# Reordering the head loads of a dense-GELU forward and backward kernel: one load queue, the activation table first, a split first run

## The chip, the cores and the metric

The kernel runs on one core of one Trainium2 chip. The metric is device microseconds of the whole program, the median of several executions. The profile's span, from the first to the last recorded instruction, is a little shorter than that time.

## The reference

One dense layer with a GELU, a second dense layer, and the gradients of both:

```python
h   = einsum("bsd,df->bsf", x, w1) + b1
out = einsum("bsf,fd->bsd", gelu_tanh(h), w2) + b2
out, vjp = jax.vjp(f, x, w1, b1, w2, b2)
return out, *vjp(grad_out)
```

Here x and grad_out are 1 x 2048 x 448, w1 is 448 x 1792 and w2 is 1792 x 448, all in bf16. The six results are the output and the gradients of x, w1, b1, w2 and b2.

## The kernel before, in words

The 2048 rows of x form four blocks of 512, and the 1792 hidden columns form seven pairs of 2 x 128 columns, so there are 28 units of (block, pair). For each unit TensorE makes u = x w1 (steps named `u<unit>.<half>`) and q = grad_out w2^T (`q`), ScalarE and VectorE make gelu, its derivative and their products, and TensorE then adds up the output (`p`, `o`) and the gradient of x (`x`). After the four blocks the gradients of w1 and w2 follow (lines 839 and 893).

Nothing is scheduled at run time: the order of each engine's work is written out by hand in `PE_ORDER`, `ACT_ORDER`, `DVE_ORDER` and `SP_ORDER` (lines 91 to 133), and the semaphores come from what each instruction reads and writes. TensorE works on two halves of its rows at once: a `run` is a list of slots, and each slot is a pair of matmuls of 64 rows each.

The head is the stretch before the first u steps flow. Its names:

- `W6` (lines 386 to 390): six matmuls of 128 x 512 on a constant, without use for the result. `F6` (lines 392 to 395): six slots of 128 columns on a constant, likewise.
- `xr01`, `xr12`, `xr24` (`LXN`, line 597): loads of x's row tile 0, of tile 1, and of tiles 2 and 3 (each tile 128 rows of 896 bytes) into a buffer of the TR group. They are plain loads; x's first block is turned by TensorE.
- `ident` (`identity`, line 602): VectorE builds a 128 x 128 identity from counted numbers, with four constants that GpSimd writes (`identz`, line 724).
- `X0` to `X3` on TensorE (`XT`, line 617): the turn of one x tile against the identity, four slots of 64 columns. `X<t>.<i>` on ScalarE and VectorE (`XC`, line 630) copies a turned half tile out of PSUM into xT.
- `L0` to `L4` (`LW1`, line 644): column parts of w1's first 384 rows; parts 0 to 3 have 256 columns, and part 4 the rest. Part 1 is loaded in two pieces, `L1a` and `L1b`. `Z0` to `Z2` (`LW1Z`, line 649) load w1's last 128 rows, by columns, into a spare area of gh_nat. `K0` to `K3` load w2, `b1` loads the bias, and `X1` in `SP_ORDER` is the transposing load of x's second block.
- `S0` (line 268): unit 0 for x's tiles 0 and 1. It is three runs one behind the other: `second(0), second(1)` (two slots), `first(0..3)` (four slots), `second(2)` (one slot), each slot 256 columns wide. The last slot of `first` and the slot of `second(2)` read the Z0 area.
- `T1` (line 716): the first half of unit 0 for x's tiles 2 and 3, one tile of 128 columns after the other. `B`: a small matmul for the bias, between S0 and T1. `k0A k0B` and `c0..` add up unit 0's pieces and take them out of PSUM. Then come `u1.1 h1.2 u1.2 u2.1 u3.1 ...`.

Two queues load in the head. ScalarE issues `xr12`, `L0` and `Z0`, and loads its Gelu table behind them (`table`, line 765). SyncE issues `xr01`, `xr24`, `b1`, `L1a`, `L1b`, `Z1`, `L2`, `L3` and so on. A hand-written dependency (`HOLD`, line 554) makes the issue of `L1a` wait until the identity has been built; all of SyncE's later issues stand behind it.

Of the kernel before, what the change touches and what calls it, by code (L numbers as in the profile page):

```python
# [9 lines left out]
ALU = mybir.AluOpType  # L10
BF16 = mybir.dt.bfloat16
F32 = mybir.dt.float32
# [76 lines left out]


PE_ORDER = """
W6 X0 X1 F6 X2 X3 S0 B T1 u1.1 h1.2 u1.2 u2.1 u3.1 u2.2 u3.2 p0.0 p0.1 p0.2 p0.3 p1.0 p1.1 p1.2 u4.1 u5.1 u4.2
u5.2 p1.3 p2.0 p2.1 p2.2 p2.3 u6.1 p3.0 u6.2 p3.1 p3.2 p3.3 p4.0 p4.1 u7.1 p4.2 u7.2 p4.3 p5.0 p5.1 p5.2 p5.3 u8.1
p6.0 u8.2 q0.1 p6.1 q0.2 u9.1 p6.2 u9.2 q1.1 p6.3 q1.2 u10.1 o1.0.0.6.1 u10.2 q2.1 o1.1.0.6.1 u11.1 q2.2 u11.2
o1.0.0.6.2 o1.1.0.6.2 q3.1 u12.1 q3.2 u12.2 o1.0.6.10.1 q4.1 o1.1.6.10.1 u13.1 q4.2 u13.2 o1.0.6.10.2 q5.1 o1.1.6.10.2
# [11 lines left out]
x3.1.6.10.1 x3.0.6.10.2 x3.1.6.10.2 x3.0.10.14.1 x3.1.10.14.1 x3.0.10.14.2 x3.1.10.14.2  # L107
"""
ACT_ORDER = """
xr12 L0 Z0 table X0.1 X1.1 X2.0 X3.0 k0A k0B c0A1 s0 g0 s1 g1 c2B t0 s2 g2 g3 s3 c5B g4 t1 t2 c6B g5 g6 s4 s5 g7 c8A c8B g8 c9A c9B  # L110
g9 c10A c10B t3 t4 g10 s6 c11A c11B s7 g11 t5 c12A c12B g12 s8 t6 c13A c13B g13 s9 t7 s10 t8 c14A c14B t9 g14 s11 s12
c15A c15B t10 g15 c16A c16B s13 t11 g16 c17A c17B s14 t12 g17 c18A c18B s15 g18 vx0.2 c19A c19B t13 t14 g19 s16 c20A
c20B s17 g20 t15 s18 t16 s19 c21A c21B t17 g21 c22A c22B s20 t18 g22 c23A c23B g23 s21 t19 s22 t20 s23 c24A c24B t21
# [12 lines left out]
vx3.3  # L126
"""
SP_ORDER = """
xr01 xr24 b1 L1a L1b Z1 L2 L3 K0 K1 L4 Z2 K2 K3 X1 R F b2 Y0 J0 J1 J2 Y1 I0 E J3 I1 So0.1 So0.0 X2 H0 H1 H2 H3 H4 H5 H6 H7 H8 H9
T0 T1 H10 T2 H11 T3 H12 T4 H13 T5 So1.0 So1.1 T6 T7 H14 T8 Y2 H15 T9 X3 H16 T10 H17 Sx0.0 Sx0.1 T11 H18 H19 T12 H20  # L130
T13 T14 T15 So2.0 Y3 H21 So2.1 T16 H22 H23 T17 T18 T19 H24 Sx1.0 T20 Sx1.1 H25 T21 H26 Nx H27 T22 T23 Sx2.0 Sx2.1 T24
T25 T26 So3.0 So3.1 Ng T27 Sx3.0 Sx3.1
# [28 lines left out]
def make_plan(tc, ctx, x, w1, b1, w2, b2, grad_out, out_0, out_1, out_2, out_3, out_4, out_5):  # L161
    nc = tc.nc
    P = 128
    _, S, D = x.shape
    F = w1.shape[1]
    NS, NF, SB = S // P, F // P, 512
# [7 lines left out]
    g2 = grad_out.rearrange("b s d -> (b s) d")  # L174
# [11 lines left out]
    w1_sb = w1f[:, 0:4 * F].rearrange("p (k f) -> p k f", k=4)  # L186
# [6 lines left out]
    xT = [sb.tile([P, 4, EDGE + SB], BF16, name=f"xT{i}") for i in range(2)]  # L193
# [14 lines left out]
    stage = [sb.tile([P, 2, D], BF16, name=f"st{i}") for i in range(NST)]  # L208
# [12 lines left out]
    pl = Plan()  # L221


    DEP = mybir.DependencyInfo(mybir.DependencyClass.Sync, mybir.DependencyReason.DATA)
# [21 lines left out]
        for i in (0, 1):  # L246
            tail_of[slots[-1][i][0], i] = (n_run[0], m, idle)

    def uq_run(w, t, banks, pair, d, c0=0, c1=SB, at=0):

        ft = (2 * (pair % NPB), 2 * (pair % NPB) + 1)

        def plain(i, k, low, st, sp, banks=banks):
            rows = slice(0, 64) if low else slice(64, 128)
            cols = slice(ft[i] * P, (ft[i] + 1) * P)
            return (banks[i], (at, c1 - c0), w[rows, k, cols] if k < 3 else w1z[rows, cols], t[rows, k, EDGE + c0:EDGE + c1], st, sp)

        if w is w1_sb and pair < NPB and d < 3:
            if d == 1:
                run([(plain(1, k, True, k + at == 0, False), plain(0, k, False, k + at == 0, False)) for k in (0, 1, 2, 3)])
            else:
                run([(plain(0, k, True, False, k == 2), plain(1, (0, 1, 3)[k], False, False, k == 2)) for k in (0, 1, 2)])
            return

        if d == 3:
            one_, two = banks[:2], banks[2:]

            def first(k):
                return [plain(1, k, True, k == 0, k == 3, one_), plain(0, k, False, k == 0, k == 3, one_)]

            def second(k):
                return [plain(0, k, True, k == 0, k == 2, two), plain(1, (0, 1, 3)[k], False, k == 0, k == 2, two)]

            run([second(0), second(1)])
            run([first(k) for k in range(4)])
            run([second(2)])
            return  # L280

        def half(i, k, low, st, sp):
            rows = slice(0, 64) if low else slice(64, 128)
            early = not low and k == 3
            a, b = EDGE + c0 - early, (0 if w is w1_sb else EDGE - early) + ft[i] * P
            return (banks[i], c1 - c0, w[rows, k, b:b + P], t[rows, k, a:a + c1 - c0], st, sp)

        if d == 1:
            run([(half(1, k + 1, True, k == 0, False), half(0, k, False, k == 0, False)) for k in (0, 1, 2)])
        else:  # L290
            run([(half(0, k, True, False, k == 3), half(1, k, False, False, k == 3)) for k in (0, 1, 2, 3)])
# [20 lines left out]
    def pe(name, fn, reads, writes, cost, pat):  # L312
        o = pl.op("PE", name, fn, reads, writes, cost)
        o["pat"] = pat
        return o
# [13 lines left out]
    def part_w1(p):  # L329
        return ("w1", W1_PART[p % NPB])  # L330

    def U(p, d, hf=None, by_tile=False):
        b = p // NPB
        if hf is None:
            bk, hs, c, tag = u_banks(p), (0, 1), (0, SB), ""
            vs = [bank(("u", p, 0), bk[0]), bank(("u", p, 1), bk[1])]
        else:
            bk, hs, c, tag = ((4, 5), (0, 1))[hf], (hf,), (256 * hf, 256 * hf + 256), f"h{hf}"
            vs = [bank(("u", p, 0, hf), bk[0]), bank(("u", p, 1, hf), bk[1])]
            if d == 3:  # L340
                bk = bk + (6, 7)
                vs += [bank(("ux", p, 0), 6), bank(("ux", p, 1), 7)]
        rd = [part_w1(p)] + [("xT", b, h) for h in hs] + ([("w1z", REST[p])] if b == 0 else ["w1r"])
        if d == 2 and b > 0:
            rd += [("xe", b), "w1f"]
        def fn():
            for a in range(c[0], c[1], P) if by_tile else (c[0],):
                uq_run(w1_sb, xT[b % 2], bk, p, d, a, a + P if by_tile else c[1], a - c[0])

        pe(f"u{p}.{d}{tag}", fn, rd, vs,  # L350
           ("s512" if hf is None else "s256", 2 + d), (bk, d))

    def Q(p, d):
# [169 lines left out]
    for i, t in enumerate([t for t in SP_ORDER.split() if t[0] == "S"]):  # L523
        b, half = t[2:].split(".")
# [25 lines left out]
    def dq(eng):  # L550
        return {"SP": nc.sync, "ACT": nc.scalar, "POOL": nc.gpsimd}[eng]

    loads = {}
    HOLD = {"w11m0": "ident"}

    def dma(eng, name, out, in_, reads, writes, nbytes):
        def fn():
            d = loads[name] = dq(eng).dma_start(out=out, in_=in_)
            if name in HOLD:
                tc.add_manual_dep(d.ins, loads[HOLD[name]].ins.name, DEP, reason="behind the identity")  # L560
        pl.op(eng, name, fn, list(reads) + (["ident"] if name in HOLD else []), writes, ("dma", nbytes, "plain"))

    def dmaT(name, out, in_, reads, writes, nbytes, eng="SP"):
        pl.op(eng, name, lambda: dq(eng).dma_start_transpose(out=out, in_=in_), reads, writes, ("dma", nbytes, "turn"))
# [26 lines left out]

    x_rows = TR[NTR - 1][:, :, :, :].rearrange("p a h s -> p (a h) s")
    ident = stage[0][:, 0, 0:P]
    nums, turned, nums128 = stage[1][:, 0, 0:16], stage[1][:, 0, 32:64], stage[1][:, 0, 128:256]
    row, block = [stage[1][:, 1, 2 * i:2 * i + 2].bitcast(F32) for i in (0, 1)]

    def LXN(t0, t1, eng="SP"):

# [2 lines left out]

    def identity():

        nc.vector.memset(nums[:, 0:1], 0.0)
        for i in range(4):
            n = 1 << i
            nc.vector.tensor_scalar(out=nums[:, n:2 * n], in0=nums[:, 0:n], scalar1=float(n), scalar2=None, op0=ALU.add)
        low = nums[:, None, 0:16].to_broadcast([P, 8, 16])
        high = nums[:, 0:8, None].to_broadcast([P, 8, 16])
        nc.vector.scalar_tensor_tensor(out=nums128.rearrange("p (a b) -> p a b", a=8), in0=high, scalar=16.0, in1=low, op0=ALU.mult, op1=ALU.add)  # L610
        nc.vector.transpose(out=turned, in_=nums128[:, 0:32])
        nc.vector.tensor_scalar(out=row, in0=turned[:, 0:1], scalar1=block, scalar2=None, op0=ALU.add)
        loads["ident"] = nc.vector.tensor_scalar(out=ident, in0=nums128, scalar1=row, scalar2=None, op0=ALU.is_equal)

    X_BANKS = ((0, 1), (2, 3), (0, 1), (2, 3))

# [74 lines left out]
    def num(t):  # L691
        return [int(i) for i in t.split(".")]

    for t in PE_ORDER.split():
        k, a = t[0], t[1:]
        if k == "w":
            wake(int(a), P)
        elif k == "W":
            wake(int(a))
        elif k == "X":  # L700
            XT(int(a))
        elif k == "f":
            fill(int(a), (3, 2), 2 * P)
        elif k == "F":
            fill(int(a), (6, 7), 2 * P)
        elif k == "B":
            pe("b1u", lambda: nc.tensor.matmul(bk_(5)[:, 256:272], lhsT=b1n[0:64, :], rhs=ident[0:64, 0:16], start=True, stop=True,  # L707
                                               skip_group_check=True), ["b1n", "b1z", "ident"], [val(("b1u",), ("bank5b",))], ("s16", 1), (None, 0))
        elif k == "d":
            DM(*num(a))  # L710
        elif k == "h":
            hf, d = num(a)
            U(0, d, hf)
        elif k == "S":
            U(0, 3, int(a))
        elif k == "T":
            U(0, 1, int(a), True)
        elif k in "uqp":
            {"u": U, "q": Q, "p": OP}[k](*num(a))
        else:  # L720
            b, half, f0, f1, d = num(a)
            UN(k, b, half, list(range(f0, f1)), d)
# [214 lines left out]
```

## Time and profile before

| what | value |
|---|---|
| time, median of 3 runs | 264.4 us (264.23 to 264.69) |
| span of the profiled execution | 262.2 us |
| TensorE busy | 258.8 us (99%) |
| VectorE busy | 199.5 us (76%) |
| ScalarE busy | 127.6 us (49%) |
| bytes moved by DMA | 46.61 MB, mean 178 GB/s |

The profiled execution has no time listed beside its span; the median of the runs lies 2.2 us above the span. In the timeline a row says when a merged group of instructions begins and how long it lasts, then engine, line, operation, the tile written and the tiles read, and the count. An entry in square brackets is the idle time before it and what ended it. Rows that end in q (SPq, ACTq) are the issuing of DMAs, not their transfer.

### The profile page before, as it was taken

Reading aid. Unit: us, or ns where it says so; the run is one execution under the profiler, and the core shown is the slowest. Engines: PE = TensorE matmul, PEld = TensorE weight load, DVE = VectorE, ACT = ScalarE, POOL = GpSimd, SP = SyncE. Lnnn points to the kernel's source line nnn. Section 1 sums busy time; section 2 is a strip of 40 time slices with the busy share of each in tenths; the row PEclk is TensorE's granted clock in tenths of the full one; section 3 lists DMA queues with packets and bytes.
Section 4 is the critical chain, followed back from the end, with each engine's and each line's share of the span. In section 5 each row is a group of like instructions: output and inputs, shape, how many; then the busy total and the mean of one; then the engine's idle time right before and its main releaser. Section 6 shows DMA issues by size and latency. Waiting matters only on the chain.

```text
span 262.2 us, 5415 instructions
## 1 busy us (share of the span) xinstructions
PE 258.8 (99%) x2217; PEld 149.5 (57%) x2217; DVE 199.5 (76%) x287; ACT 127.6 (49%) x166; POOL 14.2 (5%) x11
## 2 busy tenths in 40 slices
PE   8999999999999999999999999999999999999995
PEld 5444455555555666666666677765555555555554
DVE  5999398999989989999997995249999999310000
ACT  5899569936898956875896310011121111000001
POOL 1000000000000000000000000000000392400000
PEclk9999999999999999999999999999999999999999
DMA  6999989999999892972487824974899999975221
GB/s 201 292 249 171 197 127 197 258 341 212 244 180 220 236 228 43 195 203 43 107 203 257 216 42 63 262 211 106 162 217 136 184 213 171 235 152 158 72 70 35
DMA packets 120633, 46.61 MB, mean 178 GB/s; under 512 B 96686, under 2 KB 120479, under 8 KB 120608
## 3 DMA queue, kind: packets, MB, share of 16 engines
q1 hardware_dynamic: 119920, 45.82, 78.0%
q10 hardware_dynamic: 688, 0.44, 0.6%
q8 instruction: 17, 0.28, 0.4%
q14 instruction: 8, 0.07, 0.1%
HBM read 8.20 MB, written 14.28 MB: 86 GB/s over the span
## 4 chain that ended last, share of the span: by engine, by line
PE 99%; ACT 0%; issue 0%
PE bank L242 48%; PE qb L242 18%; PE bank L839 16%; PE bank L893 16%; PE qb L389 1%; ACT w_sb L898 0%; PE bank L707 0%
## 5 line engine op out<-in xcount | busy, mean ns | idle before, releaser
L242 PEld LDWEIGHTS <-HG 64*128 64x128 bf16 x896 | 55.7, 94 | 32.2 <-POOLq L236 2.1
L242 PE MATMUL qb<-gT,w2Tf 64*128 64x512 bf16 x392 | 52.9, 376 | 0.0
L242 PE MATMUL bank<-w_sb,HG 64*128 64x448 bf16 x448 | 48.4, 349 | 0.0
L242 PE MATMUL bank<-xT,w1f 64*128 64x512 bf16 (+2 forms) x361 | 47.3, 368 | 0.0
L242 PE MATMUL bank<-w1T_sb,HG 64*128 64x448 bf16 x448 | 47.2, 349 | 0.0
L515 DVE SCALAR_TENSOR_TENSOR HG<-TR,qb 128x1024 bf16<-128x1024 bf16 x28 | 34.1, 1217 | 12.6 <-PE qb L242 12.6
L893 PE MATMUL bank<-w2Tf,HG 128*128 128x448 bf16 (+2 forms) x240 | 42.6, 340 | 0.0
L839 PE MATMUL bank<-w1f,gh_nat 128*128 128x448 bf16 x224 | 42.5, 352 | 0.0
L893 PEld LDWEIGHTS <-HG 128*128 128x128 bf16 x240 | 22.9, 98 | 19.8
L839 PEld LDWEIGHTS <-gh_nat 128*128 128x128 bf16 x224 | 21.8, 98 | 20.6 <-issue 0.4
L242 PEld LDWEIGHTS <-w2Tf 64*128 64x128 bf16 x392 | 24.1, 94 | 16.6 <-POOLq L236 0.3
L500 ACT ACTIVATE TR<-TR 128x1024 bf16<-128x1024 bf16 x28 | 29.2, 1052 | 6.6 <-DVE TR L490 6.6
L242 PEld LDWEIGHTS <-w1f 64*128 64x128 bf16 x388 | 22.0, 94 | 17.3 <-POOLq L236 0.7
L862 DVE TENSOR_TENSOR w1T_sb<-w1T_sb,gh_nat 128x1792 f32<-128x1792 f32 x14 | 28.4, 2025 | 0.5
L844 ACT ACTIVATE TR<-bank 128x448 bf16<-128x448 f32 x14 | 7.6, 543 | 34.9 <-PE bank L839 34.9
L899 DVE CAST w_sb<-bank 128x448 bf16<-128x448 f32 x6 | 3.7, 624 | 25.9 <-PE bank L893 25.9
L898 ACT CAST w_sb<-bank 128x448 bf16<-128x448 f32 (+2 forms) x9 | 4.4, 490 | 37.7 <-PE bank L893 37.7
L868 POOL PARTITION_ALL_REDUCE w1T_sb<-w1T_sb x1 | 10.6, 10570 | 206.0 <-DVE w1T_sb L866 206.0
L475 ACT ACTIVATE TR<-gh_nat 128x1024 bf16<-128x1024 bf16 x15 | 15.7, 1052 | 11.5 <-DVE TR L510 11.5
L505 DVE TENSOR_SCALAR TR<-TR 128x2048 bf16<-128x2048 bf16 x28 | 19.2, 688 | 1.9 <-ACT TR L500 1.9
L495 DVE TENSOR_TENSOR TR<-TR,HG 128x1024 bf16<-128x1024 bf16 x28 | 19.2, 684 | 0.0
L510 DVE TENSOR_TENSOR TR<-TR 128x1024 bf16<-128x1024 bf16 x28 | 19.0, 686 | 0.1
(54 smaller groups left out, 190.6 us busy)
## 6 DMA issues: line engine op xcount, KB each, us to landing
hT_dram<-HG SPq DMA_DIRECT2D x28, 256.0 KB, 3.2
out_dram<-st SPq DMA_DIRECT2D x16, 224.0 KB, 3.3
w1f<-in_x_dram SPq DMA_DIRECT2D x2, 896.0 KB, 6.0
w2Tf<-in_grad_out_dram SPq DMA_DIRECT2D x1, 1792.0 KB
out_dram<-w_sb SPq DMA_DIRECT2D x2, 448.0 KB, 2.8
out_dram<-xT SPq DMA_DIRECT2D x2, 384.0 KB, 3.4
w_sb<-in_w_dram SPq DMA_DIRECT2D x1, 672.0 KB
w1f<-in_w_dram SPq DMA_DIRECT2D x1, 576.0 KB
```

The source lines that it names most:

```text
L242: m = nc.tensor.matmul(bk_(b)[:, at:at + n], lhsT=l, rhs=r, start=st, stop=sp, skip_group_check=True)
L475: pl.op("ACT", f"s{p}", lambda: nc.scalar.activation(out=TR[p % NTR][:, 1], in_=ubuf(p), func=ACT.Square, scale=sc), [("ub", p)], [v], ("a ...
L495: pl.op("DVE", f"R{p}", lambda: nc.vector.tensor_tensor(out=t[:, 1], in0=t[:, 1], in1=hblk(p), op=ALU.mult), [("r", p), ("h", p)], [val((" ...
L500: pl.op("ACT", f"t{p}", lambda: nc.scalar.activation(out=t[:, 0], in_=t[:, 0], func=ACT.Tanh), [("y", p)], [val(("t", p), ("TR0", p % NTR) ...
L505: pl.op("DVE", f"m{p}", lambda: nc.vector.tensor_scalar(out=t[:], in0=t[:], scalar1=1.0, scalar2=None, op0=ALU.subtract), [("t", p), ("r2" ...
L510: pl.op("DVE", f"n{p}", lambda: nc.vector.tensor_tensor(out=t[:, 0], in0=t[:, 0], in1=t[:, 1], op=ALU.mult), [("m0", p), ("m1", p)], [val( ...
L515: pl.op("DVE", f"G{p}", lambda: nc.vector.scalar_tensor_tensor(out=ghblk(p), in0=t[:, 0], scalar=2.0, in1=qb[:, :, :], op0=ALU.subtract, o ...
L839: nc.tensor.matmul(bk_(bk)[:, 0:D], lhsT=gh_nat[:, st // 4, ft, st % 4, :], rhs=x_nat[:, st, :], start=(st == 0), stop=(st == NS - 1))
L844: fn = (lambda dst=dst, src=src: nc.scalar.mul(out=dst, in_=src, mul=-0.5)) if eng == "ACT" else \
L862: nc.vector.tensor_tensor(out=hs3, in0=a, in1=gh_nat[:, st // 4, :, st % 4, :], op=ALU.add)
L868: pl.op("POOL", "gb1", lambda: nc.gpsimd.partition_all_reduce(gb1_w, hsum, channels=P, reduce_op=bass_isa.ReduceOp.add), ["hsc"], ["gb1"], ...
L893: nc.tensor.matmul(bk_(bk)[:, 0:d1 - d0], lhsT=h_nat[ft][:, st, :], rhs=g_nat[:, st, d0:d1], start=(st == 0), stop=(st == NS - 1))
```

## The change

Six edits, all in the head.

```diff
 PE_ORDER = """
-W6 X0 X1 F6 X2 X3 S0 B T1 u1.1 h1.2 ...
+W4 F1 X0 F1 X1 F4 S0.1 X2 X3 S0.2 S0.3 B T1 u1.1 h1.2 ...
 ACT_ORDER = """
-xr12 L0 Z0 table X0.1 X1.1 X2.0 X3.0 k0A k0B ...
+table Z0 X0.1 X1.1 X2.0 X3.0 k0A k0B ...
 SP_ORDER = """
-xr01 xr24 b1 L1a L1b Z1 L2 L3 K0 K1 L4 ...
+xr01 xr12 L0 xr24 b1 L1 L2 Z1 L3 K0 K1 L4 ...
...
-            run([second(0), second(1)])
-            run([first(k) for k in range(4)])
-            run([second(2)])
+            run([[second(0), second(1)], [first(k) for k in range(4)], [second(2)]][part - 1])
             return
...
-    loads = {}
-    HOLD = {"w11m0": "ident"}
...
-            d = loads[name] = dq(eng).dma_start(out=out, in_=in_)
-            if name in HOLD:
-                tc.add_manual_dep(d.ins, loads[HOLD[name]].ins.name, DEP, reason="behind the identity")
+            dq(eng).dma_start(out=out, in_=in_)
...
-        nc.vector.memset(nums[:, 0:1], 0.0)
+        def spread(out, src, n, m):
+            high = src[:, 0:n, None].to_broadcast([P, n, m])
+            low = src[:, None, 0:m].to_broadcast([P, n, m])
+            nc.vector.scalar_tensor_tensor(out=out.rearrange("p (a b) -> p a b", a=n), in0=high, scalar=float(m), in1=low, op0=ALU.mult, op1=ALU.add)
+
         for i in range(4):
-            n = 1 << i
-            nc.vector.tensor_scalar(out=nums[:, n:2 * n], in0=nums[:, 0:n], scalar1=float(n), scalar2=None, op0=ALU.add)
...
-        nc.vector.scalar_tensor_tensor(out=nums128.rearrange("p (a b) -> p a b", a=8), in0=high, scalar=16.0, in1=low, op0=ALU.mult, op1=ALU.add)
+            nc.vector.memset(nums[:, i:i + 1], float(i))
+        spread(nums16, nums, 4, 4)
+        spread(nums128, nums16, 8, 16)
         nc.vector.transpose(out=turned, in_=nums128[:, 0:32])
-        nc.vector.tensor_scalar(out=row, in0=turned[:, 0:1], scalar1=block, scalar2=None, op0=ALU.add)
-        loads["ident"] = nc.vector.tensor_scalar(out=ident, in0=nums128, scalar1=row, scalar2=None, op0=ALU.is_equal)
+        nc.vector.tensor_scalar(out=ident, in0=nums128, scalar1=block, scalar2=turned[:, 0:1], op0=ALU.subtract, op1=ALU.is_equal)
```

In words: (1) SyncE issues the loads of x tile 0, x tile 1, w1 part 0 and x tiles 2 and 3 in this order; ScalarE keeps Z0 alone, behind its table. (2) The hold of L1 on the identity goes, and L1 is one load instead of two. (3) L2 goes ahead of Z1. (4) The identity takes four constants, two `scalar_tensor_tensor`, one transpose and one comparison, with the numbers in f32 instead of bf16. (5) Four warm matmuls instead of six, and the six filling slots stand in three places instead of one. (6) S0's first run (two slots) stands ahead of the turns of x tiles 2 and 3, and its other two runs behind them. All that follows `B` is as it was.

More of the change, by code (lines that the diff above doesn't have):

```diff
@@ L91 @@
 PE_ORDER = """
-W6 X0 X1 F6 X2 X3 S0 B T1 u1.1 h1.2 u1.2 u2.1 u3.1 u2.2 u3.2 p0.0 p0.1 p0.2 p0.3 p1.0 p1.1 p1.2 u4.1 u5.1 u4.2
+W4 F1 X0 F1 X1 F4 S0.1 X2 X3 S0.2 S0.3 B T1 u1.1 h1.2 u1.2 u2.1 u3.1 u2.2 u3.2 p0.0 p0.1 p0.2 p0.3 p1.0 p1.1 p1.2 u4.1 u5.1 u4.2
 u5.2 p1.3 p2.0 p2.1 p2.2 p2.3 u6.1 p3.0 u6.2 p3.1 p3.2 p3.3 p4.0 p4.1 u7.1 p4.2 u7.2 p4.3 p5.0 p5.1 p5.2 p5.3 u8.1
@@ L109 @@
 ACT_ORDER = """
-xr12 L0 Z0 table X0.1 X1.1 X2.0 X3.0 k0A k0B c0A1 s0 g0 s1 g1 c2B t0 s2 g2 g3 s3 c5B g4 t1 t2 c6B g5 g6 s4 s5 g7 c8A c8B g8 c9A c9B
+table Z0 X0.1 X1.1 X2.0 X3.0 k0A k0B c0A1 s0 g0 s1 g1 c2B t0 s2 g2 g3 s3 c5B g4 t1 t2 c6B g5 g6 s4 s5 g7 c8A c8B g8 c9A c9B
 g9 c10A c10B t3 t4 g10 s6 c11A c11B s7 g11 t5 c12A c12B g12 s8 t6 c13A c13B g13 s9 t7 s10 t8 c14A c14B t9 g14 s11 s12
@@ L128 @@
 SP_ORDER = """
-xr01 xr24 b1 L1a L1b Z1 L2 L3 K0 K1 L4 Z2 K2 K3 X1 R F b2 Y0 J0 J1 J2 Y1 I0 E J3 I1 So0.1 So0.0 X2 H0 H1 H2 H3 H4 H5 H6 H7 H8 H9
+xr01 xr12 L0 xr24 b1 L1 L2 Z1 L3 K0 K1 L4 Z2 K2 K3 X1 R F b2 Y0 J0 J1 J2 Y1 I0 E J3 I1 So0.1 So0.0 X2 H0 H1 H2 H3 H4 H5 H6 H7 H8 H9
 T0 T1 H10 T2 H11 T3 H12 T4 H13 T5 So1.0 So1.1 T6 T7 H14 T8 Y2 H15 T9 X3 H16 T10 H17 Sx0.0 Sx0.1 T11 H18 H19 T12 H20
@@ L247, in run, with uq_run @@
             tail_of[slots[-1][i][0], i] = (n_run[0], m, idle)
-    def uq_run(w, t, banks, pair, d, c0=0, c1=SB, at=0):
+    def uq_run(w, t, banks, pair, d, c0=0, c1=SB, at=0, part=0):
         ft = (2 * (pair % NPB), 2 * (pair % NPB) + 1)
@@ L330, in part_w1, with U @@
         return ("w1", W1_PART[p % NPB])
-    def U(p, d, hf=None, by_tile=False):
+    def U(p, d, hf=None, by_tile=False, part=0):
         b = p // NPB
@@ L347, in fn @@
             for a in range(c[0], c[1], P) if by_tile else (c[0],):
-                uq_run(w1_sb, xT[b % 2], bk, p, d, a, a + P if by_tile else c[1], a - c[0])
-        pe(f"u{p}.{d}{tag}", fn, rd, vs,
+                uq_run(w1_sb, xT[b % 2], bk, p, d, a, a + P if by_tile else c[1], a - c[0], part)
+        pe(f"u{p}.{d}{tag}.{part}", fn, rd, vs,
            ("s512" if hf is None else "s256", 2 + d), (bk, d))
@@ L551, in dq @@
         return {"SP": nc.sync, "ACT": nc.scalar, "POOL": nc.gpsimd}[eng]
-    loads = {}
-    HOLD = {"w11m0": "ident"}
     def dma(eng, name, out, in_, reads, writes, nbytes):
         def fn():
-            d = loads[name] = dq(eng).dma_start(out=out, in_=in_)
-            if name in HOLD:
-                tc.add_manual_dep(d.ins, loads[HOLD[name]].ins.name, DEP, reason="behind the identity")
-        pl.op(eng, name, fn, list(reads) + (["ident"] if name in HOLD else []), writes, ("dma", nbytes, "plain"))
+            dq(eng).dma_start(out=out, in_=in_)
+        pl.op(eng, name, fn, reads, writes, ("dma", nbytes, "plain"))
     def dmaT(name, out, in_, reads, writes, nbytes, eng="SP"):
@@ L593, in make_plan @@
     ident = stage[0][:, 0, 0:P]
-    nums, turned, nums128 = stage[1][:, 0, 0:16], stage[1][:, 0, 32:64], stage[1][:, 0, 128:256]
-    row, block = [stage[1][:, 1, 2 * i:2 * i + 2].bitcast(F32) for i in (0, 1)]
+    nums, nums16, block = [stage[1][:, 0, 64 * i:64 * i + 2 * n].bitcast(F32) for i, n in ((0, 4), (1, 16), (2, 1))]
+    turned, nums128 = stage[1][:, 0, 256:320].bitcast(F32), stage[1][:, 1, 0:256].bitcast(F32)
     def LXN(t0, t1, eng="SP"):
@@ L602, in identity @@
     def identity():
-        nc.vector.memset(nums[:, 0:1], 0.0)
+        def spread(out, src, n, m):
+            high = src[:, 0:n, None].to_broadcast([P, n, m])
+            low = src[:, None, 0:m].to_broadcast([P, n, m])
+            nc.vector.scalar_tensor_tensor(out=out.rearrange("p (a b) -> p a b", a=n), in0=high, scalar=float(m), in1=low, op0=ALU.mult, op1=ALU.add)
         for i in range(4):
-            n = 1 << i
[L607 to L610, printed above, removed]
+            nc.vector.memset(nums[:, i:i + 1], float(i))
+        spread(nums16, nums, 4, 4)
+        spread(nums128, nums16, 8, 16)
         nc.vector.transpose(out=turned, in_=nums128[:, 0:32])
-        nc.vector.tensor_scalar(out=row, in0=turned[:, 0:1], scalar1=block, scalar2=None, op0=ALU.add)
-        loads["ident"] = nc.vector.tensor_scalar(out=ident, in0=nums128, scalar1=row, scalar2=None, op0=ALU.is_equal)
+        nc.vector.tensor_scalar(out=ident, in0=nums128, scalar1=block, scalar2=turned[:, 0:1], op0=ALU.subtract, op1=ALU.is_equal)
     X_BANKS = ((0, 1), (2, 3), (0, 1), (2, 3))
@@ L714, in make_plan @@
         elif k == "S":
-            U(0, 3, int(a))
+            hf, part = num(a)
+            U(0, 3, hf, part=part)
         elif k == "T":
```

## The prediction

> **What bounds the kernel now.** The page comes first: its head, and the chain that ended last.
>
> ```profile
> span 262.2 us, 5415 instructions
> ...
> PE 258.8 (99%) x2217; PEld 149.5 (57%) x2217; DVE 199.5 (76%) x287; ACT 127.6 (49%) x166; POOL 14.2 (5%) x11
> ...
> PE 99%; ACT 0%; issue 0%
> ```
>
> TensorE is on the chain for 99% of the span. So whatever brings the dense stream of matmuls forward or back moves the end by as much, and an edit of the head counts only as far as it moves that stream. Next the timeline of the head, TensorE's rows and the copies between its turns and T1:
>
> ```profile
> 0.76 2.72 PE L389 MATMUL qb<-const-bfloat16-1.0 128*128 128x512 bf16 x6 [0.76 <-PEq L921]
> ...
> 3.41 0.61 PE L242 MATMUL bank<-st,TR 64*128 64x64 bf16 x16
> ...
> 3.83 0.83 PE L242 MATMUL qb<-const-bfloat16-1.0 64*128 64x128 bf16 x12
> ...
> 4.45 0.51 PE L242 MATMUL bank<-st,TR 64*128 64x64 bf16 x16
> ...
> 4.80 0.38 PE L242 MATMUL qb<-xT,w1f 64*128 64x256 bf16 x4
> 4.88 0.65 ACT L633 CAST xT<-bank 128x256 bf16<-128x256 f32 x2 [0.36 <-PE bank L242]
> 4.98 0.76 DVE L633 CAST xT<-bank 128x256 bf16<-128x256 f32 x2 [0.39 <-PE bank L242]
> ...
> 5.56 0.35 PE L242 MATMUL bank<-xT,w1f 64*128 64x128 bf16 x6
> ...
> 5.89 0.34 PE L242 MATMUL bank<-xT,w1f 64*128 64x128 bf16 x6
> ...
> 6.11 0.83 PE L242 MATMUL bank<-xT,w1f 64*128 64x512 bf16 x6
> ...
> 7.95 0.83 PE L242 MATMUL qb<-xT,w1f 64*128 64x512 bf16 x6
> ...
> 9.00 0.33 PEld L242 LDWEIGHTS <-w1f 64*128 64x128 bf16 x6 [0.51 <-DMA w1f<-in_w_dram]
> 9.01 0.82 PE L242 MATMUL bank<-xT,w1f 64*128 64x512 bf16 x6
> ```
>
> These are the warm matmuls, X0 and X1, F6, X2 and X3 (4.45), S0 (4.80), T1's two tiles (5.56 and 5.89), u1.1 (6.11), u2.1 (7.95) and u3.1 (9.01). Before u3.1 the weights came late. The chain in order of time has u2.1 and u3.1, eight matmuls each:
>
> ```profile
> 8.12 0.86 PE qb L242 x8
> 9.01 1.04 PE bank L242 x8
> ```
>
> u3.1 takes 0.2 us more, which it loses to L3; without that it would start at 7.95 + 0.86 = 8.81. Behind it the chain is TensorE to the end. Two things are thus worth time: when u1.1 starts, and the 0.2 us at L3.
>
> What sets u1.1? T1's second tile at 5.89, and it waits for VectorE's second copy, which ends at 4.98 + 0.76 = 5.74. The copies wait for X2 and X3, and those for x's last tiles. The loads, first their issues, then the time from issue to landing (last column, us):
>
> ```profile
> 0.72 0.87 SPq L558 DMA_DIRECT2D TR<-in_x_dram  x2
> ...
> 1.15 0.47 ACTq L558 DMA_DIRECT2D w1f<-in_w_dram  x1
> ...
> 1.64 0.53 ACTq L558 DMA_DIRECT2D gh_nat<-in_w_dram  x1
> ...
> 2.91 0.91 SPq L558 DMA_DIRECT2D w1f<-in_w_dram  x2
> ...
> 4.34 0.98 SPq L558 DMA_DIRECT2D w1f<-in_w_dram  x2
> ```
>
> ```profile
> TR<-in_x_dram SPq DMA_DIRECT2D x1, 224.0 KB, 3.1
> w1f<-in_w_dram ACTq DMA_DIRECT2D x1, 192.0 KB, 3.5
> ...
> gh_nat<-in_w_dram ACTq DMA_DIRECT2D x1, 128.0 KB, 3.4
> ...
> TR<-in_x_dram SPq DMA_DIRECT2D x1, 112.0 KB, 2.5
> ```
>
> ```profile
> w1f<-in_w_dram SPq DMA_DIRECT2D x1, 192.0 KB, 4.1
> ```
>
> x's last tiles are issued at 0.72 + 0.44 = 1.16 and land at 4.3. Tile 0 lands at 3.2, L0 at 4.65, Z0 at 5.04, and L3 (issued second of its pair, 4.83) at 8.93. X2 starts at 4.45, 0.2 us behind its data, held by F6.
>
> ```profile
> core 0: us, PE busy (x) PEld busy (x) DVE busy (x) ACT busy (x) POOL busy (x), PEclk, DMA share, GB/s
> ...
> 2.40:4.40 2.00, 2.00 (x31) 1.15 (x31) 1.01 (x4) 1.82 (x4) 0.00 (x0) 1.00 1.03 328
> 4.40:6.00 1.60, 1.60 (x50) 1.44 (x46) 1.13 (x4) 0.78 (x4) 0.00 (x0) 1.00 0.83 223
> 6.00:9.00 3.00, 2.99 (x36) 1.50 (x32) 2.13 (x5) 2.19 (x4) 0.00 (x0) 1.00 0.94 254
> ```
>
> From 2.4 to 4.4 us the 16 DMA engines are full (1.03); from 4.4 to 6 they are not (0.83), because SyncE's second group of issues begins only at 2.91, behind the identity.
>
> **The change, part by part.**
>
> *Order of the loads.* Today SyncE's queue holds tile 0 and the last tiles, while ScalarE's holds tile 1, L0 and Z0; both are served in turns, so the last tiles share only with the first part of ScalarE's list. In one queue they come fourth: 112 + 112 + 192 KB go ahead. Z0's 128 KB, in the other queue, is served in turns with them and so falls ahead of their end too, whether ScalarE issues it at once (about 0.8) or behind the table and its activation (about 2.2). So the last tiles land when all 768 KB are in. Today the same 768 KB are in at 5.04, together with a little of L1. Bounds: 4.3, if the order cost nothing, and 5.04. I take 4.9, near the upper end, since the engines are full and their bytes are the same. That is 0.6 later than now.
>
> *From X2 to u1.1.* Now 6.11 - 4.45 = 1.66 us. The copies set it: the first VectorE copy 0.53 behind X2's start, two copies 0.76, the hand-over 0.15, T1's second tile 0.22. At X2 TensorE still runs slowly: F6's six slots of 128 columns are (0.83 - 0.31)/5 = 0.10 us apart, with 0.31 for one matmul (next row), while S0's seven slots of 256 columns, from 4.80 to 5.56, are 0.108 apart. At full speed X2's four slots give back 0.1, so 1.56.
>
> ```profile
> L242 PE MATMUL qb<-const-bfloat16-1.0 64*128 64x128 bf16 x12 | 0.8, 308 | 0.0
> ```
>
> *S0 split.* S0's seven slots lie beside the copies. Two of them move ahead of X2, into a wait for data (L0 is ahead of the last tiles in the queue). TensorE then has 8 turn slots of 0.03, five of 0.108 and B, 0.8 us, before T1; T1's second tile can't start before 0.53 + 0.76 + 0.15 = 1.44. The two slots come off a path that isn't last: 0. They would be worth up to 0.2 if the copies were faster.
>
> So X2 starts at 4.95 (0.05 for the hand-over, as from L3's landing at 8.93 to 9.00) and u1.1 at 4.95 + 1.56 = 6.5: **+0.4**.
>
> *The hold on L1, and L2 before Z1.* SyncE issues every 0.44 to 0.5 us. Tile 0, tile 1, L0, last tiles, bias, L1, L2, Z1, L3 put L3's issue at 0.72 + 8 x 0.46 = 4.4, against 4.83. The engines' gap of 1.6 x 0.17 = 0.27 us goes as well, so L3 lands at 8.5 to 8.7. u3.1 asks for it at 8.81 + 0.4 = 9.2. The wait goes: **-0.2**. The cover is 0.5 us; were it gone, the 0.2 stays. All later loads are issued some 0.4 earlier, the transposing one of x's second block too, and TensorE waits for none of them today.
>
> *Identity.* From these rows:
>
> ```profile
> 0.79 0.06 DVE L604 MEMSET st<- 128x1 bf16 x1 [0.79 <-PEq L921]
> 0.89 0.81 DVE L607 TENSOR_SCALAR st<-st 128x1 bf16<-128x1 bf16 x4
> ...
> 1.73 0.29 DVE L610 SCALAR_TENSOR_TENSOR st<-st 128x128 bf16<-128x128 bf16 x1
> ...
> 2.06 0.21 DVE L611 STREAM_TRANSPOSE st<-st 128x32 bf16<-128x32 bf16 x1
> 2.21 1.28 ACT L765 ACT_TABLE_LOAD   x1 [2.21 <-issue]
> ...
> 2.63 0.25 DVE L613 TENSOR_SCALAR st<-st 128x128 bf16<-128x128 bf16 x1
> ```
>
> Four constants 0.24, two spreads 0.2 to 0.3 each, transpose 0.21, comparison 0.25 to 0.3, hand-overs 0.2: ready at about 2.2 (at 2.9 if f32 doubled all), against 2.88. X0's data come at 2.7 to 3.2: hidden, 0. The table, 1.28 us from 0.7 on, is done long before the first copy: 0, as now (3.5, first copy 3.88). Two warm matmuls fewer end in a wait for tile 0; the fillers are moved, not added: 0 as long as the clock isn't touched (below).
>
> *Sum:* +0.4 - 0.2 = +0.2 us on the span of 262.2. What lies around the span, 2.2 us against the median of the runs (264.4), is untouched: **264.6 us**, no change that can be told. About 0.2%, 0.53 us, is the least that a measurement of this kernel tells from none.
>
> **The rivals.**
>
> *Data earlier (faster).* If the engines, no longer split at the start, bring the last tiles at 4.3 or sooner, then X2 starts at 4.35 without F6 in front, u1.1 at 5.9 to 6.0, and L3's 0.2 goes: -0.3 to -0.4; with 4.05, still at the slow clock, 4.1 + 1.66 = 5.76, -0.35 - 0.2 = -0.55: 263.9 us. For it: from 1.6 to 2.4 the engines are not yet full. Against it: Z0's bytes still share. Chance 0.25, and 0.15 that it passes the bound.
>
> *One queue fills the engines less (slower).* With both queues working they moved 328 GB/s, with SyncE's alone 254 (6 to 9 us). The 786,000 bytes then take up to 0.7 us longer; last tiles at 5.5, u1.1 +1.0, L3 -0.2: 265.2 us. Against it: 6 to 9 us has other row sizes, and 0.94 of the engines is busy there. It decides from about 5.2 on. Chance 0.13.
>
> *The clock stays low (slower).* The profile's column shows a granted 1.00 throughout, yet the time per column halves between F6 and S0 (above), so about 3.9 us after the first matmul at 0.76. Today TensorE has no gap in these 3.9 us. After the change W4 and one filler end at 2.6, and tile 0 comes at 2.7 to 3.2; a second hole opens before X2. If what lifts the clock counts anew from X0 (3.2), full speed comes at 7.1: from X2 to there the work runs at half speed, about 1.0 us lost behind what the copies hide, so +1.0 + 0.2: 265.6 us. Chance 0.12. The Trainium skill ("TensorE: Matmul & The Clock Gate", Part 1) has this as a rule that speaks against fewer warm matmuls: the clock is halved until one window of some 3.4 us was busy throughout, and the windows run freely. The 3.9 us agree; no trace here shows how much of a hole a window forgives.
>
> **How the numbers follow.** Forecast 0.50 (within 0.2%), data earlier 0.25 (0.15 faster, 0.10 within), lower filling 0.13 and clock 0.12 (both slower). So faster 0.15, same 0.60, slower 0.25. The range goes down to 263.8 (data at 4.05, and a little for the run) and up to 265.3: it holds the forecast's own, 264.0 to 264.8 from the bounds 4.3 and 5.04, and the lower filling, and leaves out most of the clock's case.
>
> **What would show it.** Right: TR's last load lands at 4.7 to 5.0, X2 starts behind it after a hole on TensorE, u1.1 starts near 6.5, and u3.1's weights have no idle time by a DMA. The prediction is wrong if X2 starts before 4.5 (data earlier), if S0's slots of 256 columns are 0.2 us apart (clock), if the DMA share from 2.4 to 4.4 falls to 0.9 or less, or if TensorE, with u1.1 later and L3 no longer in the way, shows new waits behind 9 us.

## The result, and the profile after

The changed kernel takes 266.55 us (266.44 to 267.63, 4 executions) against 264.54 us (264.23 to 264.73) for the kernel before: ratio 1.0089, interval 1.0066 to 1.0112. (A ratio is taken over all executions, and is not the quotient of the two medians.) It is slower by about 2.0 to 2.4 us, where 264.6 us was forecast in a range of 263.8 to 265.3. The profiled execution took 266.44 us with a span of 264.7 us.

The page after, its head and its chain:

```profile
span 264.7 us, 5411 instructions
...
PE 259.7 (98%) x2215; PEld 149.4 (56%) x2215; DVE 199.0 (75%) x286; ACT 127.7 (48%) x166; POOL 14.2 (5%) x11
...
PE 97%; DMA 2%; SPq 0%; ACT 0%; issue 0%
```

A share of the chain has gone from TensorE to a DMA. The timeline of the head, TensorE and the issues:

```profile
0.72 1.28 ACT L761 ACT_TABLE_LOAD   x1 [0.72 <-PEq L917]
...
0.76 1.86 PE L387 MATMUL qb<-const-bfloat16-1.0 128*128 128x512 bf16 x4 [0.76 <-PEq L917]
0.78 0.37 ACTq L554 DMA_DIRECT2D gh_nat<-in_w_dram  x1
...
1.63 0.43 SPq L554 DMA_DIRECT2D w1f<-in_w_dram  x1
1.83 0.35 DVE L608 TENSOR_SCALAR st<-st 128x128 bf16<-128x128 f32 x1
...
2.11 0.49 SPq L554 DMA_DIRECT2D TR<-in_x_dram  x1
...
3.19 0.39 PE L242 MATMUL bank<-st,TR 64*128 64x64 bf16 x8 [0.35 <-DMA TR<-in_x_dram]
...
3.85 0.62 PE L242 MATMUL qb<-const-bfloat16-1.0 64*128 64x128 bf16 x8
...
5.65 0.61 PE L242 MATMUL qb<-xT,w1f 64*128 64x256 bf16 x4 [1.19 <-DMA w1f<-in_w_dram]
6.26 0.45 PEld L242 LDWEIGHTS <-TR 64*128 64x128 bf16 x16 [0.48 <-DMA TR<-in_x_dram]
6.26 0.61 PE L242 MATMUL bank<-st,TR 64*128 64x64 bf16 x16
...
6.68 0.83 PE L242 MATMUL bank<-xT,w1f 64*128 64x256 bf16 x6
...
8.59 0.90 PE L242 MATMUL bank<-xT,w1f 64*128 64x512 bf16 x6
...
11.38 0.82 PE L242 MATMUL bank<-xT,w1f 64*128 64x512 bf16 x6
```

SyncE's issues follow each other by some 0.47 us, so L0 is issued at 1.63 and the last tiles only at 2.11, where the kernel before issued them at 1.15 and 1.16 from two queues. TensorE stands still for 1.19 us ahead of S0's first run (5.65), since L0 is late; X2 starts at 6.26 instead of 4.45; six matmuls of 256 columns then take 0.83 us; and u1.1 starts at 8.59 instead of 6.11, 2.48 us later. u3.1 starts at 11.38 instead of 9.01, without a wait for its weights. No new wait follows, and the span is 2.45 us longer. All of the loss lies ahead of u1.1: 1.81 us before X2, and 0.67 us between X2 and u1.1 (2.33 instead of 1.66).

The loads (from issue to landing, last column), and the windows in which the DMA engines should have been full:

```profile
TR<-in_x_dram SPq DMA_DIRECT2D x1, 224.0 KB, 4.1
w1f<-in_w_dram SPq DMA_DIRECT2D x1, 192.0 KB, 4.0
gh_nat<-in_w_dram ACTq DMA_DIRECT2D x1, 128.0 KB, 2.5
```

```profile
2.40:3.20 0.80, 0.45 (x5) 0.12 (x4) 0.00 (x0) 0.00 (x0) 0.00 (x0) 1.00 0.97 330
3.20:4.20 1.00, 1.00 (x26) 0.84 (x26) 0.55 (x2) 0.47 (x2) 0.00 (x0) 1.00 0.29 58
4.20:6.00 1.80, 0.61 (x10) 0.13 (x4) 0.30 (x1) 0.28 (x1) 0.00 (x0) 1.00 1.03 317
```

L0 lands at 1.63 + 4.0 = 5.6 (before 4.65) and the last tiles at 2.11 + 4.1 = 6.2 (before 1.16 + 3.1 = 4.3). Of the 2.0 us that the last tiles lose, 0.95 is the later issue and 1.0 the longer way from issue to landing. Between 3.2 and 4.2 us the engines move 58 GB/s at a share of 0.29; the kernel before moved 343 in the same stretch:

```profile
3.20:4.20 1.00, 1.00 (x25) 0.79 (x26) 0.36 (x2) 0.82 (x4) 0.00 (x0) 1.00 1.10 343
```

That is some 285,000 bytes less in a stretch in which TensorE's next steps wait for loads that were issued at 1.63 and 2.11.

### The profile page after: what moved, and what is told of

It is laid out like the page before. It is cut to its first block, busy times and chain, and to the rows that moved or that the text cites. A ratio compares the mean times of both kernels' runs of the same rounds, so it can differ in the third digit from the quotient of the medians.

```text
span 264.7 us, 5411 instructions
## 1 busy us (share of the span) xinstructions
PE 259.7 (98%) x2215; PEld 149.4 (56%) x2215; DVE 199.0 (75%) x286; ACT 127.7 (48%) x166; POOL 14.2 (5%) x11
## 4 chain that ended last, share of the span: by engine, by line
PE 97%; DMA 2%; SPq 0%; ACT 0%; issue 0%
PE bank L242 47%; PE qb L242 17%; PE bank L835 16%; PE bank L889 16%; DMA w1f<-in_w_dram 2%; SPq L554 0%; ACT w_sb L894 0%; PE bank L702 0%
## 5 line engine op out<-in xcount | busy, mean ns | idle before, releaser
L242 PE MATMUL bank<-xT,w1f 64*128 64x512 bf16 (+2 forms) x361 | 48.0, 373 | 0.0
L242 PEld LDWEIGHTS <-w1f 64*128 64x128 bf16 x388 | 22.6, 97 | 18.4 <-DMA w1f<-in_w_dram 1.4
```

The lines of the kernel that those rows point to most:

```text
L242: m = nc.tensor.matmul(bk_(b)[:, at:at + n], lhsT=l, rhs=r, start=st, stop=sp, skip_group_check=True)
```

## The experiments

Two theories were tried first. A: the loads' order costs the time, and the slow clock follows from the hole that it makes. B: the clock is late because only four warm matmuls are left. Ratios are to the kernel before, run beside each. A profile shows one execution: in the four runs whose head loads are those of the kernel after, L0 landed between 5.3 and 5.9 and the last tiles between 5.9 and 6.5.

**Loads back.** The kernel after, with the loads' queues as before:

```diff
-table Z0 X0.1 X1.1 ...
+xr12 L0 Z0 table X0.1 X1.1 ...
-xr01 xr12 L0 xr24 b1 L1 ...
+xr01 xr24 b1 L1 ...
```

> The kernel after, with only the queues of the head loads as before (ScalarE: tile 1, L0, Z0, then the table; SyncE: tile 0, last tiles, bias, L1 and so on). Theory A (the loads' order costs the time: L0 begins slowly, as it does in both traces, and in one queue it holds x's last tiles back; the late clock only follows from the hole that TensorE then has): the last tiles land near 4.3 us and L0 near 4.7, S0's first run starts near 4.75, X2 near 5.0, the clock is up by then or soon after, u1.1 starts near 6.6, and the time is 264.4 to 265.0 us. Theory B (the clock is late because only four warm matmuls are left, whatever the loads do): from X2 to u1.1 it still takes 2.3 us instead of 1.6, u1.1 near 7.4, time 265.4 to 265.8 us.

265.87 us, 264.78 to 266.91 over 8 executions; ratio 1.0061 (1.0039 to 1.0084). The time is neither theory's, just above B's. L0 landed at 5.3 and the last tiles at 5.0 here, and S0's first run, which now stands ahead of X2, made X2 wait for L0 (X2 5.71). From X2 to u1.1 it took 2.35 us, so the clock was slow here as well. The edits of TensorE's order are no better without the new loads: they cost time of their own.

**Loads only.** The kernel after, with TensorE's order as before:

```diff
-W4 F1 X0 F1 X1 F4 S0.1 X2 X3 S0.2 S0.3 B T1 ...
+W6 X0 X1 F6 X2 X3 S0.1 S0.2 S0.3 B T1 ...
```

> The kernel after, with TensorE's order as before (six warm matmuls, six fillers in one place, S0 behind the turns of the last tiles). Theory A: the loads still land as in the kernel after (L0 5.6, last tiles 6.2), so X2 starts at 6.2 to 6.3 and the time stays above 265.8 us; S0 in one piece adds 0 to 0.4 us if the clock is slow. Theory B: with six warm matmuls the clock is up at about 4.7 us, from X2 to u1.1 it takes 1.6 us instead of 2.3, time 265.7 to 265.9 us, while the loads are as late. If the clock is late here too, the wait on the loads, not the number of warm matmuls, delays it.

265.52 us; ratio 1.0058 (1.0040 to 1.0075). TensorE's rows, of an execution at the median:

```profile
6.20 0.41 PE L242 MATMUL bank<-st,TR 64*128 64x64 bf16 x16 [1.46 <-DMA TR<-in_x_dram]
...
6.66 0.49 PE L242 MATMUL bank<-xT,w1f 64*128 64x256 bf16 x6
...
7.75 0.83 PE L242 MATMUL bank<-xT,w1f 64*128 64x512 bf16 x6
```

X2 is as late as in the kernel after, yet from X2 to u1.1 it takes 1.55 us: the clock is up. So the loads alone (with the short identity and the missing hold, which stay in) cost 1.5 us, by the lateness of the data. The engines moved 149 GB/s at a share of 0.65 from 3.2 to 4.2 us here, more than twice the kernel after's 58, and yet the last tiles landed as late, at 6.15.

**L0 in three loads** of 128 rows each, one behind the other in the same place (`xr01 xr12 L0a L0b L0c xr24 ...`).

> The kernel after, with L0 as three loads of 128 rows instead of one of 384 (same bytes, same place in the queue). Theory A1 (a load with three pieces per partition starts late, by the making of its descriptors): the DMA engines are no longer nearly idle from 3.2 to 4.2 us, the last tiles land near 4.9 us, time 264.6 to 265.4 us. Theory A2 (the first reading of these rows of w1 is slow, however it is cut): the share of the DMA engines from 3.2 to 4.2 us stays below 0.5, the last tiles land at 6.2 us or later, time 266.3 to 267.2 us.

267.35 us, ratio 1.0111 (1.0080 to 1.0143): the time is in the range of A2, the landings are not. The three pieces, issued at 1.64, 2.11 and 2.58, had all landed at 4.8, 0.8 us ahead of the one load issued at 1.63. But the last tiles were now issued at 3.11 and landed at 5.8, and TensorE had three holes (0.33, 0.18 and 0.54 us). Cutting makes L0 come earlier, and the issues it adds (0.47 us each) are paid by what follows.

**Holes filled.** The kernel after with 27 fillers: `W4 F6 X0 F3 X1 F18 S0.1 X2 ...`.

> The kernel after, with 27 filling slots in place of six in the same three places, so that TensorE has hardly a hole before S0. The loads do not change under either theory. If the holes delay the clock: full speed again near 4.7 us, from X2 to u1.1 some 1.6 us instead of 2.3, u1.1 near 7.9 us instead of 8.6, time 265.8 us. If the clock has another reason: 266.5 us, as the kernel after.

265.71 us (265.60 to 265.73); ratio 1.0052 (1.0037 to 1.0067), 0.8 us less than the kernel after, and the four executions agree within 0.13 us. The loads were as late (engines at 105 GB/s from 3.2 to 4.2 us):

```profile
3.94 2.11 PE L242 MATMUL qb<-const-bfloat16-1.0 64*128 64x128 bf16 x36
5.84 0.64 PE L242 MATMUL qb<-xT,w1f 64*128 64x256 bf16 x4
6.26 0.60 PE L242 MATMUL bank<-st,TR 64*128 64x64 bf16 x16
6.70 0.49 PE L242 MATMUL bank<-xT,w1f 64*128 64x256 bf16 x6
...
7.94 0.83 PE L242 MATMUL bank<-xT,w1f 64*128 64x512 bf16 x6
```

X2 still starts at the slow clock, but S0 (6.70) is at the full one: u1.1 at 7.94, 0.65 us earlier than in the kernel after with the same X2. Useless work in the holes gave back what the late clock cost here. Full speed came at about 6.6, not at 4.7 as expected.

**The hold alone.** The kernel before with `HOLD = {}`.

> The kernel before with one edit: L1's loads no longer wait for the identity. Theory H (the wait was worth its time: it keeps L1's bytes off the loads that are needed first): L0, in the other queue, lands at 5.0 to 5.3 us instead of 4.7 and the last tiles at 4.5 or later instead of 4.2; S0 starts 0.3 to 0.6 us later, the 0.2 us that L3 costs goes, and the time is 0.1 to 0.5 us more than that of the kernel before. Rival (the prediction's step): L1 stands behind the last tiles in the same queue and takes nothing from them; L3 lands earlier, 0.2 us less.

264.22 us beside 264.04; ratio 1.0006 (0.9996 to 1.0017): no difference that can be told. L0 landed at 4.7 and the last tiles at 4.4, Z0 0.2 us later; L3 still landed at 8.8, only 0.1 earlier. The prediction's gain of 0.2 us isn't there; theory H's late L0 isn't there either, though a cost of up to 0.45 us isn't excluded.

**Four warm matmuls alone.** The kernel before with `W4` for `W6`.

> The kernel before with one edit: four warm matmuls instead of six. The loads are the same under both theories; TensorE has a hole of about 0.8 us between 2.6 and 3.4 us. Clock theory (a stretch of about 3.4 us has to be busy throughout, and a hole spoils the one it falls into): the clock lifts some 1 to 3 us later in part of the executions, so the median is 0.3 to 1.0 us more and the spread is wider than the 1.0 us of the kernel before. Rival (one short hole is forgiven): the same time within 0.15 us and the same spread.

264.80 us, 264.32 to 265.77; ratio 1.0027 (1.0012 to 1.0042). The loads landed as before, and X2 started at 4.35, yet u1.1 at 7.12 instead of 6.11:

```profile
3.31 0.61 PE L242 MATMUL bank<-st,TR 64*128 64x64 bf16 x16 [0.68 <-DMA TR<-in_x_dram]
...
5.21 0.84 PE L242 MATMUL bank<-xT,w1f 64*128 64x256 bf16 x6
...
7.12 1.04 PE L242 MATMUL bank<-xT,w1f 64*128 64x512 bf16 x6
```

S0 and T1 run at half speed: 0.84 for the six matmuls that take 0.49 at full speed. In this profile u1.1 comes 1.0 us later, but one profile can't put that down to the hole of 0.68 us ahead of X0, for a kernel without a hole can have the clock as late (the rest only, below). The executions can: they take 0.3 to 1.1 us more by the interval.

**Last tiles ahead of L0** in the one queue (`xr01 xr12 xr24 L0 ...`), TensorE's order as before.

> As the run in which only the loads are those of the kernel after (TensorE's order as before), but x's last tiles go ahead of L0 in the one queue. Theory A1 (a load with three pieces per partition is slow to begin, and what stands behind it in its queue waits): the last tiles land at 4.2 to 4.5 us instead of 6.15, L0 lands at 5.3 to 5.8, S0 starts then, u1.1 near 6.7 to 7.0, time 264.5 to 264.9 us. Rival (the queue runs dry from 3.2 to 4.2 us whatever stands there): the last tiles land at 5 us or later, time as that run, 265.5 us or more.

265.93 us, ratio 1.0063 (1.0039 to 1.0088). The rival is nearer: the last tiles landed at 5.0 and L0 at 5.6, and the engines moved 206 GB/s from 3.2 to 4.2. A load with three pieces per partition isn't the whole cause. Counted from their issues (1.63 and 2.10), the last tiles took 3.4 us and L0 3.5, against 3.1 and 3.55 in the kernel before: here most of the lateness is the late issue. The profile is of the faster half of the executions (three at 264.93 to 265.34, three at 266.52 to 266.56).

**L0 on ScalarE's queue**, ahead of Z0 (`table L0 Z0`; `xr01 xr12 xr24 b1 ...`).

> As the run in which only the loads are those of the kernel after, but L0 goes to ScalarE's queue, ahead of Z0, and SyncE's queue has tile 0, tile 1, last tiles. Theory A1: L0's slow start is hidden behind x's tiles in the other queue; the DMA engines have no idle stretch from 3.2 to 4.2 us, the last tiles land at 4.2 to 4.6 us, L0 at 4.2 to 4.8, u1.1 at 6.0 to 6.5, time 264.0 to 264.5 us. Rival (L1, no longer held, takes the gain): L0 or Z0 lands at 5.2 us or later, time 264.6 to 265.2 us.

264.87 us, ratio 1.0047 (1.0025 to 1.0070); eight executions at 264.49 to 265.10 and four at 266.51 to 266.92. L0 landed at 3.9, the earliest of all, and no stretch was empty after 2.4 us; but the last tiles came at 5.3. The last tiles, issued at 1.62, took 3.7 us: L0, no longer late, shares the engines with them.

**One load more.** As loads only, with K0 (224 KB of w2) behind Z0 on ScalarE's queue.

> As the run in which only the loads are those of the kernel after (six warm matmuls, TensorE's order as before), but K0, 224 KB of w2 that nobody needs before 10 us, is issued on ScalarE's queue behind Z0, at about 1.2 us. Theory D (the engines run dry near 3 us because the third load of one queue is not ready, and are slow to start again; what keeps them fed mends it): the DMA engines move over 250 GB/s throughout from 2.4 to 4.4 us, and L0 lands no later than 5.3 us and the last tiles no later than 6.0, although 224 KB more stand beside them. Theory E (the descriptors of L0 and of the loads behind it in its queue are late by themselves): L0 lands at 5.4 us or later and the last tiles at 6.2 or later, as without K0, since K0 only fills the gap. Time 265.2 to 265.8 us by either; the landings tell.

The windows, the same three as above:

```profile
2.40:3.20 0.80, 0.80 (x3) 0.15 (x1) 0.00 (x0) 0.00 (x0) 0.00 (x0) 1.00 1.06 345
3.20:4.20 1.00, 0.78 (x19) 0.41 (x20) 0.36 (x1) 0.33 (x1) 0.00 (x0) 1.00 1.09 354
4.20:6.00 1.80, 0.53 (x24) 0.36 (x18) 0.49 (x2) 0.42 (x2) 0.00 (x0) 1.00 1.07 325
```

The engines are full throughout, and L0 (5.2) and the last tiles (5.9) land no later, although 224 KB more came in beside them. So L0 and the last tiles didn't lack engines in the empty stretch: it was capacity that SyncE's loads left unused. The landings are on theory D's side of its bounds, but the run with the holes filled had 5.3 and 5.9 without K0, so this doesn't settle D against E. The time was 266.92 us: ratio 1.0102 (1.0074 to 1.0129). The profile is of the one execution of four at 265.25; the others took 266.90 or more.

**Same order, two queues:** `xr12 xr24 Z0 table` on ScalarE, `xr01 L0 b1 L1 ...` on SyncE, TensorE's order as before.

> The loads of the kernel after in the same order of need, but over two queues: SyncE has tile 0, L0, bias, L1 and so on, ScalarE has tile 1, the last tiles, Z0, then the table. TensorE's order as before. If one queue is the cause (its third load isn't ready when the engines ask for it): no idle stretch, L0 at 4.2 to 4.8 us, last tiles at 4.2 to 4.7, u1.1 at 6.0 to 6.5, time 263.9 to 264.5 us. If the order itself is the cause: L0 or the last tiles land at 5.0 us or later, time 264.8 us or more.

264.60 us, ratio 1.0028 (1.0015 to 1.0041): half of the loss of loads only. The last tiles landed at 4.9 and L0 at 5.1, between the two cases. The issues:

```profile
0.72 0.90 ACTq L554 DMA_DIRECT2D TR<-in_x_dram  x2
1.17 0.42 SPq L554 DMA_DIRECT2D w1f<-in_w_dram  x1
```

The last tiles (second of the first row, 1.16) are issued 0.9 us earlier than in loads only, and L0 0.46; they land 1.2 and 0.4 us earlier, and the time is 0.9 us less. So what the second queue gains is nearly its earlier issues. From issue to landing the two loads still take 3.8 and 4.0 us, where the kernel before has 3.1 and 3.55.

**The rest only.** The kernel after with the old queues and TensorE's old order.

> The kernel after with the loads' queues and TensorE's order as before. What is left of the change: the short identity, no hold on L1, L1 as one load, L2 ahead of Z1. Theory: these cost and bring nothing that can be told, 264.0 to 264.3 us beside 264.05. Rival: part of the loss is theirs (L1 whole, issued at 2.2 us, takes bytes from L0 and the last tiles, as the run with the queues as before suggested with L0 at 5.3): 264.5 us or more.

264.36 us beside 263.94; ratio 1.0009 (0.9999 to 1.0020): no difference that can be told, though a cost of up to 0.5 us isn't excluded. Its profile, the slowest of the twelve executions (264.74 us), has a late clock although TensorE has no hole ahead of u1.1:

```profile
4.45 0.64 PE L242 MATMUL bank<-st,TR 64*128 64x64 bf16 x16
...
5.30 0.85 PE L242 MATMUL bank<-xT,w1f 64*128 64x256 bf16 x6
...
6.98 0.82 PE L242 MATMUL bank<-xT,w1f 64*128 64x512 bf16 x6
```

Its single matmuls become short at 6.6 us; in the kernel before they do so at 4.7, and in the hold alone at 3.8. The time of full speed differs by almost 3 us between executions of kernels without a hole.

**The split, with six warm matmuls.** The kernel after with `W6 X0 X1 F6 S0.1 X2 X3 S0.2 S0.3`.

> The kernel after with six warm matmuls and the six fillers in one place, as before; the loads and the split of S0 stay as in the kernel after. Beside the run in which only the loads were changed (265.5 us) this differs by the split alone, beside the kernel after (266.55 us) by the warm matmuls and fillers alone. The prediction's step (the split's two slots come off a path that isn't last): 265.3 to 265.7 us, L0 near 5.5, X2 near 6.2, from X2 to u1.1 some 1.6 us. Rival (S0's two slots between two waits make the clock late even with six warm matmuls): from X2 to u1.1 some 2.3 us, time over 266.2 us.

266.65 us, ratio 1.0089 (1.0067 to 1.0110): five executions at 266.53 to 266.94, one at 265.45. Six warm matmuls, with a hole of 1.15 us behind them, are no faster than four (266.55), and the profile has the late clock:

```profile
3.93 0.83 PE L242 MATMUL qb<-const-bfloat16-1.0 64*128 64x128 bf16 x12
5.91 0.61 PE L242 MATMUL qb<-xT,w1f 64*128 64x256 bf16 x4 [1.15 <-DMA w1f<-in_w_dram]
6.52 0.61 PE L242 MATMUL bank<-st,TR 64*128 64x64 bf16 x16
6.94 0.82 PE L242 MATMUL bank<-xT,w1f 64*128 64x256 bf16 x6
```

Loads only has a hole of 1.46 us, and six of its seven executions lie at 265.29 to 265.68 and one at 266.86. So both kernels have both groups of executions, some 1.3 us apart, in different shares (five of six slow here, one of seven there). The two intervals overlap; that the split moves the share is suggested, but not shown.

## Why the prediction was wrong, by its own steps

- **What bounds the kernel: right.** u1.1 moved by 2.48 us and the span by 2.45; nothing behind it took up or added anything.
- **Order of the loads: the step that failed.** It took the engines as full until all 768 KB are in, so that the last tiles land between 4.3 and 5.04. They landed at 6.2, 2.0 us later than before. Half of that is a term that the sum put at nothing: in one queue the loads are issued one behind the other, so the last tiles are issued at 2.11 instead of 1.16. The prediction uses this spacing of 0.46 for L3, but not here; with the 3.1 us from issue to landing of the kernel before, it gives 5.2, already beyond the upper bound. The other half is that landing took 4.1 us from issue instead of 3.1. The engines weren't full: from 3.2 to 4.2 us their share was 0.29, because tile 0, tile 1 and Z0 were all but in by then, and of L0, issued at 1.63, little had come yet. L0 was slow in the kernel before too: 2.5 us after its issue 157 of its 384 packets (those of 512 bytes) had begun in the trace before, 104 in the trace after, and 161 to 225 in the other three runs with the same loads. But before, SyncE's queue had two early loads beside the small bias and ScalarE's three, all issued by 1.64, and the others filled the engines meanwhile. The rival "one queue fills the engines less" named this, but took its rate from a stretch in which many loads are queued (254 GB/s), and gave +0.8 us instead of the 1.5 of the run with the loads only.
- **From X2 to u1.1: wrong by the clock.** 2.33 us instead of 1.56; where the clock was up, 1.56 was right (1.56 in the hold alone, 1.55 in loads only). The rival "the clock stays low" had a chance of 0.12, and the runs speak for its mechanism: the fillers alone gave back 0.8 us, and W4 alone cost 0.27%. But it was priced as an alternative to late data. Late data make holes in TensorE's work, so the two came together. Full speed came between 8.59 and 8.9, not at the 7.1 that it reckoned from X0. Two of the prediction's signs of being wrong came together: S0's slots of 256 columns are 0.21 us apart (7.30 and 7.52 in the trace), and the DMA share from 2.4 to 4.4 us is 0.61.
- **S0 split and warm matmuls: 0 forecast, wrong together.** With the old queues, TensorE's new order took 265.87 us (loads back) where the old order took 264.36 (the rest only); the intervals of their ratios lie apart. W4 alone cost 0.27% in the kernel before; what the split and the moved fillers cost singly isn't settled. Where the data are late, S0's first run stands ahead of X2 and waits for L0 itself.
- **The hold and L3: the wait went, but not for the reason given.** L3 landed at 8.87 instead of 8.96, not at 8.5 to 8.7. u3.1 no longer waits because it asks 2.4 us later. The hold alone brought nothing that can be told.
- **Identity and table: 0, right.** The identity was ready at 1.83 + 0.35 = 2.18, 1.0 us ahead of X0. ScalarE issued Z0 at 0.78 while the table was loading from 0.72 to 2.00, so its queue doesn't stand behind the table; of the two cases the early one holds.

The runs give a table of two by two. Against the kernel before, the rest of the change alone costs 0.09% (not told from nothing), the rest with the new loads 0.58%, the rest with TensorE's new order 0.61%, and the whole change 0.89%. Either part is worth some 0.5% alone, and only 0.3% when the other is there already: they overlap. That both act through TensorE's waits and the late clock behind them is the likely reason, not a shown one.

Two rules of the Trainium skill bear on this. "DMA: Bandwidth & Descriptors", section "Issuing engines are not separate DMA queues", says that issuing from several engines only saves the sequencer's time of issue. The two queues agree with it to some 0.3 us: last tiles issued 0.9 us earlier landed 1.2 us earlier, and the time fell from 265.52 to 264.60 us. What was wrong was to take that saving as nothing. "TensorE: Matmul & The Clock Gate", Part 1, asks for a busy window of about 3.4 us, at a phase that the kernel doesn't set. The phase fits in so far as, without a hole, full speed came 3.0 to 5.9 us after the first matmul (the hold alone and the rest only, by the durations of the single matmuls); 3.0 is shorter than that window. On holes the profiles are divided. In W4 alone, the kernel after, loads back, L0 in three loads and the split with six warm matmuls, full speed came 3.2 to 4.4 us after the last hole. In loads only, last tiles ahead of L0, L0 on ScalarE's queue and the two queues, it came within 1.2 us after the end of a hole of 0.3 to 1.5 us. So a hole doesn't always start the count anew.

**What stays open.** Why landing took up to 1.0 us longer from issue: a slow beginning of L0 fits (three small loads came sooner than one large), but no run tells it from a slow start of engines that have run dry. And what decides which executions find the clock early.

## What to carry to other kernels

When loads move into one queue, write down when each will be issued, and add the time from issue to landing that the trace shows; here 0.95 us of later issue was left out. Full DMA engines with two queues don't promise full engines with one: look at which load could fill a gap. A rival that is caused by another rival is no alternative to it; price them together. At a kernel's start, useless matmuls in the holes can be worth their place: filling them gave back 0.8 us here, and leaving one of 0.7 us cost 0.3 to 1.1 us. One profile doesn't show what a hole costs, since the clock comes at another time in each execution; compare many executions.

## What the runs showed of the hardware that was not expected

- A load of 192 KB issued third in SyncE's queue took 4.0 us to land (3.7 to 4.2 in the other three runs with these loads), three of 64 KB in its place 2.2 to 2.7 us each. It took 3.55 us as ScalarE's second load in the kernel before and 3.1 us as ScalarE's first.
- In several runs with holes in TensorE's head the executions fall into two groups with 1.1 to 1.7 us between them (264.49 to 265.10 and 266.51 to 266.92 in the run with L0 on ScalarE's queue), while the kernel before stays within 1.2 us in all its executions.
- Without a hole, TensorE's full speed came anywhere from 3.8 us (the hold alone) to 6.6 us (the rest only), with the first matmul at 0.76 in both.
